# Gated recurrence and mixture of experts on one core: a newly planned order of instructions, wider products, other fillers

## The chip, the cores and the metric

One core of a Trainium2 chip runs the whole program. The metric is the time of one execution on the device, in microseconds (us), as the median of several runs.

## What is computed

```python
# attention: B, H, S, D = 4, 8, 768, 48; complex decay a_re + i a_im, its size held under 0.999
for t in range(S):
    S_re, S_im = ar * S_re - ai * S_im + kv(t), ar * S_im + ai * S_re      # a 48 x 48 state per head
    y[t] = q[t] @ S_re
# experts: x = y as 3072 rows of 384
do = x @ w_skip > 0;  e = argmax(x @ w_gate);  gate = softmax(x @ w_gate)[e]     # 8 experts
out = x + do * gate * (relu(x @ w1[e]) @ w2[e])                            # 384 -> 1024 -> 384
```

## The kernel before

**Attention.** The sequence is cut into 6 chunks of 128 tokens; with 4 batches that gives 24 units (chunk c, batch b), each for all 8 heads. Instead of the recurrence step by step, a unit uses prefix products of the decays. `gates` (L267) takes logarithm, arctangent, exponential and sine on ScalarE, in 7 groups of units (`STARTS`), since these functions need two sets of tables and each change of set is a table load (L790). Its tiles: `tr` is the angle, which TensorE sums over the tokens with a triangular matrix (prefix product `pt`, L331); the sum, in turns, is rounded to whole turns by adding a large constant (the first rounding, `near`, L335, on ScalarE), and VectorE subtracts that (L340) and takes the absolute value (L350), so that sine and cosine (`cs`) have a small argument. `pl` (L366) is the prefix product of the logarithms, and `e` the two exponentials of it. `ready` (L407) multiplies q and k by `e` (L421) and by sine and cosine (`w`, L428), and TensorE transposes the result (`tp`, L436; copied out as `wT`, L445). `unit` (L451) makes the scores `pa` (L477), masks them into `at` (L484), the state product `ps` (L498) that is added to the state `T` (L504), the attention product `py` of scores and state (L519, L522), its copy `yT` and the output product `px` (L536), whose weights `wg` bring the rows back to 384 columns and append eight gate scores and the skip score: 105 columns for each pair of heads.

**Route.** For chunks 0 to 4 `route` (L588) finds the expert of each token and its rank there: VectorE steps, the counts `pr` on TensorE (L605 to L608), and `cand` (L633), which reads the counts back. `pr`, `ps` and `px` take turns in one PSUM bank (`ps_g`): a product for it can start only when the reader of the one before has finished. GpSimd then scatters the rows to a buffer sorted by expert, 224 places for each (L585). The last chunk has a short cut, unit by unit (`route1`, L656): its rows for expert 0 are gathered by products with one-hot tiles (`ohx`, L881), which give `pt` of the expert stage. Two small products (`pg` and `pf`, L391 and L401) carry the chunk's whole decay to the layout of the state; VectorE copies it to `Fall` (L405).

**Experts.** For each expert (`experts`, L855): gather its rows by a load (`xg`, L889), transpose (`pt`, L901), split into a high half `xh` (L907) and a low half `xl` (L911); first layer `ph`, 8 blocks of 128, each with 9 matmuls high by high, high by low and low by high (L925); ReLU on ScalarE (`hh`, L931), its low half on VectorE (`hl`, L935); second layer `po`, for two halves a and b of the rows and 8 blocks, 3 matmuls each (L946 to L948; the last one reads `hl`); scaled result `og` (L954) and a scatter by GpSimd (L958). Weights come by `weights` (L825): seven loads `r` (L841), the cast to a high half on ScalarE (`h`, L848), the subtraction to a low half on VectorE (`l`, L853). Two raw buffers serve the first two experts; a buffer is free when the subtraction has read it. `check` (L975) sets flags for inputs that need a general path; its VectorE steps (L982 to L1003) give `fb`.

**The order.** Every step is put down with its engine, a cost, a due time (in units, moved by a table `SHIFT` of one number for a kind of step), what it needs, and the buffers that it takes and frees. `Plan.order` (L73) goes through them as a list scheduler: it takes the step that can start first on its engine, among equals the one due first, and so writes out the whole program's order for TensorE (P), ScalarE (A), VectorE (V), GpSimd (G) and the loads on SyncE (S). Each engine runs its list strictly in that order. Where TensorE would have a gap before the first attention product, fillers (`warm`, L753, products of 128 by 128 whose result is not used) are put in: as many as the planned gap holds at 0.23, not before `FILL`. `warm` also doubles the cost of TensorE's steps where the plan takes the array for not yet warmed up.

## Time and profile before

| | us |
|---|---|
| median of 3 runs (412.81 to 412.97) | 412.95 |
| profiled execution, its own time | 414.31 |
| its span, first to last instruction | 412.5 |
| TensorE busy (matmuls) | 379.5 (92%) |
| VectorE busy | 317.3 (77%) |
| ScalarE busy | 278.7 (68%) |
| GpSimd busy | 64.3 (16%) |

The profiled execution takes 414.31 us, 1.8 us more than its span. Busy time is an average over stages: up to about 250 us attention, from 267 us on the experts. TensorE's matmuls overlap, so its share is an upper value. The mean granted clock of TensorE is 0.987 of full speed.

### The profile page before, as it was taken

The page shows a single profiled execution, that of the slowest core. Times are in us where ns is not written, and L with a number is a line of the kernel's source. Part 1 is how long each engine was busy: PE and PEld are TensorE (multiplying, and loading weights), DVE is VectorE, ACT ScalarE, POOL GpSimd, SP SyncE. Part 2 cuts the span into 40 slices and gives each one's busy share as a digit, 9 for nine tenths or more (in the row PEclk, how much of TensorE's full clock was granted, in tenths as well). Part 3 has the DMA queues.
Part 4 walks back from the last instruction along what each step waited for, and adds up shares of the span by engine and source line. Part 5 has one row for each costly group of instructions (what it writes and reads, how often), then busy time and mean ns, then how long its engine had stood idle before and what let it go on. Part 6 is the DMA issues. An engine that isn't in the chain of part 4 may idle for free. (4 is left out here: it accounts for less than half of the span.)

```text
span 412.5 us, 9865 instructions
## 1 busy us (share of the span) xinstructions
PE 379.5 (92%) x3742; PEld 341.0 (83%) x3742; DVE 317.3 (77%) x728; ACT 278.7 (68%) x546; POOL 64.3 (16%) x102
## 2 busy tenths in 40 slices
PE   6589999999998999899989988799999999999993
PEld 6377688678797878778968877799899999999992
DVE  5559999999999969988997977959675667757220
ACT  5797999998995799489797664447544656446020
POOL 9100000004004100520040040302112121110101
PEclk9699999999999999999999999999999999999998
DMA  9978969989869737433734765588877767771001
GB/s 157 186 120 163 184 124 167 222 246 224 157 153 203 149 74 167 102 79 70 162 88 118 208 185 173 169 264 272 245 222 225 221 200 241 214 229 64 27 2 35
DMA packets 160758, 67.15 MB, mean 163 GB/s; under 512 B 142310, under 2 KB 156295, under 8 KB 160704
## 3 DMA queue, kind: packets, MB, share of 16 engines
q1 hardware_dynamic: 158144, 61.81, 64.5%
q0 software_dynamic: 2560, 4.63, 3.4%
q8 instruction: 32, 0.52, 0.5%
q14 instruction: 22, 0.18, 0.2%
HBM read 54.24 MB, written 14.98 MB: 168 GB/s over the span
## 5 line engine op out<-in xcount | busy, mean ns | idle before, releaser
L848 ACT CAST h<-r 128x768 fp32r<-128x768 f32 (+1 forms) x56 | 51.1, 925 | 39.6 <-PE po L948 19.3
L853 DVE TENSOR_TENSOR l<-r,h 128x768 fp32r<-128x768 f32 (+1 forms) x56 | 58.8, 1070 | 14.2 <-ACT h L848 14.2
L585 POOL DMA_INDIRECT xs<-xa,sl x24 | 31.3, 1304 | 221.9 <-DVE ain L307 84.4
L436 PE MATMUL tp<-ident,w 128*96 128x128 f32 x384 | 52.2, 275 | 2.4 <-DVE w L428 1.7
L925 PE MATMUL ph<-xh,h 128*128 128x224 f32 x192 | 52.7, 279 | 1.7 <-DVE hl L935 1.4
L445 ACT COPY wT<-tp 96x512 f32<-96x512 f32 x92 | 50.4, 583 | 4.3 <-PE tp L436 4.1
L925 PE MATMUL ph<-xh,l 128*128 128x224 f32 x192 | 51.9, 274 | 0.0
L925 PE MATMUL ph<-xl,h 128*128 128x224 f32 x192 | 50.1, 275 | 0.0
L436 PEld LDWEIGHTS tp<-ident,w 128*96 128x96 f32 x384 | 41.4, 128 | 8.6 <-issue 3.7
L931 ACT ACTIVATE hh<-ph 128x224 fp32r<-128x224 f32 x64 | 22.7, 359 | 33.8 <-PE ph L925 33.8
L428 DVE TENSOR_TENSOR w<-qk,cs 128x768 f32<-128x768 f32 x48 | 44.9, 949 | 0.2
L946 PE MATMUL po<-h,hh 128*112 128x384 f32 x128 | 43.6, 341 | 0.0
L947 PE MATMUL po<-l,hh 128*112 128x384 f32 x128 | 43.1, 337 | 0.0
L948 PE MATMUL po<-h,hl 128*112 128x384 f32 x128 | 43.1, 337 | 0.0
L477 PE MATMUL pa<-wT,wT 96*64 96x128 f32 (+1 forms) x768 | 38.7, 250 | 1.1 <-issue 0.6
L925 PEld LDWEIGHTS ph<-xh,h 128*128 128x128 f32 x192 | 36.8, 192 | 2.8 <-DVE hl L935 2.1
L925 PEld LDWEIGHTS ph<-xh,l 128*128 128x128 f32 x192 | 36.8, 192 | 0.0
L519 PE MATMUL py<-at,vt 128*64 128x128 f32 x192 | 36.3, 279 | 0.6 <-DVE at L484 0.5
L935 DVE SCALAR_TENSOR_TENSOR hl<-ph,hh 128x224 fp32r<-128x224 f32 x64 | 23.6, 383 | 16.4 <-ACT hh L931 16.4
L477 PEld LDWEIGHTS pa<-wT,wT 96*64 96x64 f32 x768 | 34.1, 137 | 2.4 <-issue 1.5
L519 PE MATMUL py<-at,vs 128*64 128x128 f32 x192 | 36.1, 278 | 0.0
L925 PEld LDWEIGHTS ph<-xl,h 128*128 128x128 f32 x192 | 35.5, 192 | 0.0
(170 smaller groups left out, 849.4 us busy)
## 6 DMA issues: line engine op xcount, KB each, us to landing
r<-in_moe_w_dram SPq DMA_DIRECT2D x24, 512.0 KB
r<-in_moe_w_dram SPq DMA_DIRECT2D x32, 384.0 KB
ain<-in_a_re_dram SPq DMA_DIRECT2D x24, 192.0 KB
ain<-in_a_im_dram SPq DMA_DIRECT2D x24, 192.0 KB
qk<-in_q_dram SPq DMA_DIRECT2D x24, 192.0 KB
qk<-in_k_dram SPq DMA_DIRECT2D x24, 192.0 KB
vt<-in_v_dram SPq DMA_DIRECT2D x24, 192.0 KB
out_dram<-xa SPq DMA_DIRECT2D x5, 768.0 KB
```

Of the source, the lines that this page charges most:

```text
L428: V.tensor_tensor(n, X["qk", u][:, k].unsqueeze(2).to_broadcast([128, H, 2, D]), X["cs", c][:, b], ALU.mult)
L436: nc.tensor.transpose(tp[:, h], n[:, hh * 4 + h].rearrange("p k d -> p (k d)"), self.ident)
L445: (V.tensor_copy if onV else A.copy)(X["wT", u, k][:, hh * 4:hh * 4 + 4], X["tp", u, k, hh])
L477: PE.matmul(pa[p, i, t0:], k[:, h, ts], q[:, h, t0:], start=True, stop=True)
L519: PE.matmul(py[j * 64:j * 64 + 64, hp], vs[:, hp] if j else vt[:, 2 * hp], at[:, 2 * hp + j], start=True, stop=(c == 0))
L585: self.nc.gpsimd.indirect_dma_start(out=self.xsv[c * B + b], out_offset=bass.IndirectOffsetOnAxis(ap=sl, axis=0), in_=xa[:, b], in_offset= ...
L848: nc.scalar.copy(X["W", e, n][0][:, ks], X["raw", e, i])
L853: nc.vector.tensor_tensor(lo[:, ks], X["raw", e, i], hi[:, ks], ALU.subtract)
L925: PE.matmul(ph, w[:, k, ks(j)], x[:, k], start=(i == 0), stop=(i == len(terms) - 1))
L946: PE.matmul(po, hh[:, j, ts(t)], w2h[:, j], start=(j == 0), stop=False)
L947: PE.matmul(po, hh[:, j, ts(t)], w2l[:, j], start=False, stop=False)
L948: PE.matmul(po, hl[:, j, ts(t)], w2h[:, j], start=False, stop=(j == NF - 1))
```

## The change

It gives the planner other numbers and a few other rules, and with them a new order of nearly all instructions; and it alters some shapes.

- All constants of the planner are new: lead times of the table sets (`LEADS`, `TRIG`), of the loads and of `ready` (`READY`, `PULL`), the place of the flags (`CHECK`), and `SHIFT`, with 51 entries for 36. The cost of a score product is 0.69 for 0.62.
- Fillers may start at 3.0 instead of 9.0; a gap is counted with 0.7 less instead of 0.25 less, and the first block gets 8 fewer. The doubling of costs for an array not warmed up ends at 6.5 instead of 15.0.
- The state product has 64 columns instead of 48 (the 16 added ones are zeros of the value tile `vt`), the output product 128 instead of 105 (23 columns of zero weights). What is read from their tiles stays the same.
- The first rounding of units 0, 1 and 2 is a VectorE operation instead of one of ScalarE.
- The casts of expert 1's weights wait for the second low half `xl` of expert 0's rows, and are due from n − 0.8 in steps of 0.2, instead of from n − 1.5 in steps of 0.15 (n = 24 units). The weights of expert 0 are spread up to n − 1.25 instead of n − 0.2.
- All four scatters of the first chunk, not the first alone, name the clearing of the buffer as a need.

```diff
@@ -26,15 +26,17 @@
-AHEAD, TRIG, READY, PULL = 3.0, 1.48, 1.28, 2.95
+AHEAD, TRIG, READY, PULL = 3.0, 1.7, 1.02, 3.16
-WAFTER, WGAP, CHECK = 0.41, 0.29, 3
-FETCH = 1.69
-FILL = 9.0
-SHIFT = {'rt4': 1.08, 'xl': 0.32, 'py': -0.87, 're2': -0.04,
...
+WAFTER, WGAP, CHECK = 0.9, 0.32, 0.5
+FETCH = 1.68
+FILL = 3.0
+NV = 3
+EARLY = 1.25
+SHIFT = {'sum': -0.3, 'near': 0.18, 'qe': 1.37, 'eps': 0.48,
...
-LEADS = {0: 7.67, 1: 3.67, 2: 2.09, 3: 2.19, 4: 3.21, 5: 1.9, 6: 1.57, 7: 2.34}
+LEADS = {0: 5.86, 1: 2.7, 2: 1.89, 3: 1.23, 4: 2.34, 5: 2.24, 6: 2.0, 7: 0.84}
@@ -117,7 +119,8 @@
-            n = int((s - max(free["P"], FILL) - 0.25) / 0.23)
+            gap = s - max(free["P"], FILL) - 0.7
+            n = int(gap / 0.23) - 8 * (free["P"] < FILL)
             if e == "P" and n > 0 and ("py", 0, 0) not in end:
                 out.append((max(free["P"], FILL), ("fill", len(out)), lambda n=n: self.fill(n)))
@@ -130,7 +133,7 @@
-                    if s < FILL + 6.0 or warm[1] < 4.0:
+                    if s < 6.5 or warm[1] < 4.0:
                         us *= 2
@@ -212,7 +215,7 @@
-        self.wg = cst.tile([128, H // 2, 2 * D + E + 1], F32, name="wg")
+        self.wg = cst.tile([128, H // 2, 128], F32, name="wg")
@@ -330,9 +333,14 @@
-        @add(("near", u), "A", 0.49, t1, [("pt", u)])
-        def _():
-            A.activation(X["tr", u][:, 1], X["pt", u], AF.Copy, bias=ROUND)
+        onV = u < NV
+
+        @add(("near", u), "V" if onV else "A", 0.55 if onV else 0.49, t1, [("pt", u)])
+        def _():
+            if onV:
+                V.tensor_scalar(X["tr", u][:, 1], X["pt", u], ROUND, None, ALU.add)
+            else:
+                A.activation(X["tr", u][:, 1], X["pt", u], AF.Copy, bias=ROUND)
@@ -465,7 +473,7 @@
-            @add(("pa", u, hh), "P", 0.62, t, [("wT", u, k, hh) for k in range(2)], take=[("pa", u, hh)], free=[("wT1", u)])
+            @add(("pa", u, hh), "P", 0.69, t, [("wT", u, k, hh) for k in range(2)], take=[("pa", u, hh)], free=[("wT1", u)])
@@ -493,17 +501,17 @@
-                ps = X["ps", u] = self.ps_g.tile([96, H, D], F32, name=f"ps_{nm}", tag="g")
+                ps = X["ps", u] = self.ps_g.tile([96, H, 64], F32, name=f"ps_{nm}", tag="g")
                 for h in range(H):
-                    PE.matmul(ps[:, h], X["w", u, 1][:, h].rearrange("p k d -> p (k d)"), X["vt", u][0][:, h, 0:D], start=True, stop=True)
+                    PE.matmul(ps[:, h], X["w", u, 1][:, h].rearrange("p k d -> p (k d)"), X["vt", u][0][:, h], start=True, stop=True)
...
-                    V.tensor_tensor(T, X["Sb", u][:, :, 0:D], X["ps", u], ALU.add)
+                    V.tensor_tensor(T, X["Sb", u][:, :, 0:D], X["ps", u][:, :, 0:D], ALU.add)
@@ -528,9 +536,9 @@
-        @add(("px", u), "P", 0.925, t, [("yT", u), ("wg", 0)], take=[bank], free=[("yT", u)])
-        def _():
-            xs = [H // 2, 2 * D + E + 1]
+        @add(("px", u), "P", 0.95, t, [("yT", u), ("wg", 0)], take=[bank], free=[("yT", u)])
+        def _():
+            xs = [H // 2, 128]
...
@@ -639,7 +647,8 @@
-            steps[20] += (("zero", 4),)
+            for i in range(20, 20 + B):
+                steps[i] += (("zero", 4),)
@@ -818,11 +827,11 @@
-        gap = (n - 0.2 - t) / 8
+        gap = (n - EARLY - t) / 8
         self.weights(0, t, gap, gone, end)
         self.experts()
 
-    def weights(self, e, t, gap, need=(), begin=None):
+    def weights(self, e, t, gap, need=(), begin=None, hold=()):
@@ -840,7 +849,7 @@
-            @add(("wh", e, i), "A", 1.05 if i < KD else 0.835, t + gap * (i + 0.4), [("wd", e, i)] + old)
+            @add(("wh", e, i), "A", 1.05 if i < KD else 0.835, t + gap * (i + 0.4), [("wd", e, i)] + old + list(hold))
@@ -862,7 +871,7 @@
-        self.weights(1, n - 1.5, 0.15, [("w", u, 1)])
+        self.weights(1, n - 0.8, 0.2, [("w", u, 1)], hold=[(None, ("xl", 0, 1))])
```

Left out of the diff: the columns of `wg` and of the output product are named up to 105 where they are loaded and summed. In the trace every 32-bit product of attention is two matmuls, so that a filler counts twice there; in the lists below it counts once.

**TensorE, start of the program.** `pt` and `pl` are the prefix products of units 0, 1, 2, `tp` the first transposes. Before:

```order
L753 MATMUL warm<-turns 128x128 x22
L331 MATMUL pt_269<-tr_202,turns 128x384
L331 MATMUL pt_276<-tr_211,turns 128x384
L753 MATMUL warm<-turns 128x128
L331 MATMUL pt_285<-tr_223,turns 128x384
L366 MATMUL pl_295<-U_221,mask 128x384
L753 MATMUL warm<-turns 128x128
L366 MATMUL pl_308<-U_235,mask 128x384
L753 MATMUL warm<-turns 128x128 x16
L366 MATMUL pl_350<-U_242,mask 128x384
L753 MATMUL warm<-turns 128x128 x5
```

After:

```order
L762 MATMUL warm<-turns 128x128 x38
L334 MATMUL pt_289<-tr_202,turns 128x384
L334 MATMUL pt_292<-tr_211,turns 128x384
L334 MATMUL pt_297<-tr_223,turns 128x384
L374 MATMUL pl_311<-U_221,mask 128x384
L374 MATMUL pl_323<-U_235,mask 128x384
L762 MATMUL warm<-turns 128x128 x10
L374 MATMUL pl_351<-U_242,mask 128x384
L762 MATMUL warm<-turns 128x128
L444 MATMUL tp_0_0_370<-ident,w_0_359 96x128 x4
```

The first block of fillers grows from 22 to 38, the three `pt` stand together, and no filler stands between `pt` and `pl`.

**TensorE, after the counts of the third chunk** (`pr`, the last of its products). Before:

```order
L608 MATMUL pr_2310<-oh_2211,ones 128x8
L436 MATMUL tp_14_0_2316<-ident,w_14_2188 96x128 x4
L436 MATMUL tp_14_1_2325<-ident,w_14_2188 96x128 x4
L536 MATMUL px_0_2337<-wg,yT_0_2290 128x105 x4
L436 MATMUL tp_15_0_2353<-ident,w_15_2295 96x128 x4
L436 MATMUL tp_15_1_2363<-ident,w_15_2295 96x128 x4
```

After (left out: the scores `pa`, six rows):

```order
L616 MATMUL pr_2187<-oh_2155,ones 128x8
L444 MATMUL tp_13_1_2194<-ident,w_13_2099 96x128 x4
L485 MATMUL pa_162<-wT_12_1996,wT_12_2086 64x128
...
L444 MATMUL tp_14_0_2241<-ident,w_14_2168 96x128 x4
L444 MATMUL tp_14_1_2250<-ident,w_14_2168 96x128 x4
L506 MATMUL ps_1_2260<-vt_158,w_13_2099 96x64 x8
L527 MATMUL py_0_2279<-at_0_2271,vt_156 64x128
```

The next product for the bank of the counts was `px`, behind two transposes; it is now the state product `ps`, behind three half transposes and both scores.

**VectorE, last routing steps and first expert** (`todo` is the last step of the routing; `Fall` belongs to `pf`). Before:

```order
L718 SCALAR_TENSOR_TENSOR todo<-m_3_3651 128x1
L853 TENSOR_TENSOR l_1_3737<-r_1_2_3748,h_1_3736 128x1024
L405 COPY Fall<-pf_3693 96x32
L911 TENSOR_TENSOR xl_3775<-pt_0_3728,xh_3774 128x3x112
L911 TENSOR_TENSOR xl_3775<-pt_1_3732,xh_3774 128x3x112
L982 MEMSET ok 128x384
L995 TENSOR_SCALAR ok<-Fall 96x192
L996 TENSOR_SCALAR ok<-Fall 96x192
L853 TENSOR_TENSOR l_1_3783<-r_1_3_3764,h_1_3782 128x768
L935 SCALAR_TENSOR_TENSOR hl_3817<-ph_0_3785,hh_3816 128x224
```

After (left out: seven further steps of the flags):

```order
L727 SCALAR_TENSOR_TENSOR todo<-m_3_3658 128x1
L991 MEMSET ok 128x384
L1004 TENSOR_SCALAR ok<-Fall 96x192
L1005 TENSOR_SCALAR ok<-Fall 96x192
...
L1011 TENSOR_REDUCE fl<-todo 128x1
L920 TENSOR_TENSOR xl_3766<-pt_0_3722,xh_3765 128x3x112
L920 TENSOR_TENSOR xl_3766<-pt_1_3726,xh_3765 128x3x112
L1012 TENSOR_TENSOR fb<-fb,fl 128x1
L862 TENSOR_TENSOR l_1_3775<-r_1_0_3720,h_1_3774 128x1024
L862 TENSOR_TENSOR l_1_3775<-r_1_1_3730,h_1_3774 128x1024
L944 SCALAR_TENSOR_TENSOR hl_3807<-ph_0_3778,hh_3806 128x224
```

The subtractions `l_1` of expert 1's weights went behind the low halves `xl`, the flags (`ok` to `fl`) ahead of them, and `Fall` stands several steps earlier. In the same place of ScalarE's list the casts of the third and fourth part of expert 1's weights stand between the activations of blocks 3 and 4 of expert 0, where they were ahead of the first block; on SyncE's list the loads of these parts stand behind three gathers `xg` instead of ahead of them; and on TensorE `pg` and `pf` stand ahead of the last gathers by product, not between them and the first `ph`.

In the experts TensorE's list ran through the blocks of the first layer and then through those of the second; now second-layer products stand among them, for instance `ph` 4 and 5, `po` a3, a4, b0, a5, b1, `ph` 6, `po` b2, b3, a6, `ph` 7, and the last five products of the program are b4, b5, a7, b6, b7, so that the two results `og` are ready one right after the other.

## Rows read from the trace of the kernel before

**Rows 1.** Busy time of each engine by stretch (start:end, length; us and instructions), clock, DMA.

```profile
25.36:60.00 34.64, 32.02 (x310) 26.04 (x311) 34.22 (x66) 32.16 (x65) 0.00 (x0) 1.00 0.86 150
60.00:140.00 80.00, 76.30 (x927) 64.47 (x924) 76.40 (x183) 71.61 (x144) 10.28 (x10) 1.00 0.90 196
140.00:240.00 100.00, 95.53 (x1164) 81.94 (x1163) 87.94 (x212) 80.22 (x160) 14.58 (x11) 1.00 0.52 120
...
300.00:405.40 105.40, 105.38 (x771) 104.31 (x769) 60.68 (x105) 45.74 (x90) 15.11 (x17) 1.00 0.53 160
```

**Rows 2.** The same view, of shorter stretches; granted clock behind the engines.

```profile
13.00:19.80 6.80, 4.80 (x9) 2.89 (x10) 2.54 (x6) 4.76 (x10) 0.00 (x0) 0.50 1.44 187
...
252.00:258.00 6.00, 4.14 (x53) 3.84 (x52) 4.00 (x24) 2.84 (x5) 0.97 (x1) 1.00 0.60 195
```

**Rows 3.** Timeline of TensorE at the start: start, length, line, tiles, [idle before].

```profile
2.74 6.79 PE L753 MATMUL warm<-turns 128*128 128x128 f32 x44 [2.74 <-POOL turns L170]
14.99 2.93 PE L331 MATMUL pt<-tr,turns 128*128 128x384 f32 x4 [5.47 <-ACT tr L260]
...
21.61 3.73 PE L753 MATMUL warm<-turns 128*128 128x128 f32 x32
...
38.70 0.91 PE L331 MATMUL pt<-tr,turns 128*128 128x384 f32 x2 [0.15 <-ACT tr L260]
```

**Rows 4.** Timeline of VectorE at the start.

```profile
17.29 0.61 DVE L340 SCALAR_TENSOR_TENSOR tr<-tr,col,pt 128x384 f32<-128x384 f32 x1 [3.59 <-ACT tr L335]
18.01 0.36 DVE L350 TENSOR_SCALAR tr<-tr 128x384 int32<-128x384 int32 x1
...
25.36 0.56 DVE L293 TENSOR_TENSOR tr<-ain,tr 128x384 f32<-128x384 f32 x1 [4.08 <-ACT tr L260]
...
28.30 0.55 DVE L307 SCALAR_TENSOR_TENSOR ain<-ain,tr 128x384 f32<-128x384 f32 x1
```

**Rows 5.** Timeline of ScalarE at the start.

```profile
22.01 1.28 ACT L790 ACT_TABLE_LOAD   x1
```

**Rows 6.** Timeline of TensorE: state product, output product, scores.

```profile
44.27 1.56 PE L498 MATMUL ps<-vt,w 128*96 128x48 f32 x16 [0.18 <-DVE T L506]
...
241.70 1.04 PE L536 MATMUL px<-wg,yT 128*128 128x105 f32 x8
...
123.93 1.55 PE L477 MATMUL pa<-wT,wT 96*64 96x64 f32 x32
```

**Rows 7.** Waits of TensorE: engine, line, awaited operation: us in total, times, longest.

```profile
PE px L536 <- DVE cand L633: 2.0, 2, 1.4
...
PE ph L925 <- DVE hl L935: 1.4, 2, 0.9
```

**Rows 8.** Timelines of VectorE, TensorE, SyncE and ScalarE, from attention to experts.

```profile
262.06 1.22 DVE L853 TENSOR_TENSOR l<-r,h 128x1024 fp32r<-128x1024 f32 x1
...
263.99 1.56 PE L881 MATMUL pt<-early,xa 128*128 128x112 f32 x12 [0.18 <-DVE ohs L680]
...
266.79 0.37 PE L925 MATMUL ph<-xh,h 128*128 128x224 f32 x1 [0.32 <-ACT xh L907]
...
271.39 16.88 SPq L841 DMA_DIRECT2D r<-in_moe_w_dram  x11
...
277.57 0.83 ACT L848 CAST h<-r 128x768 fp32r<-128x768 f32 x1 [2.03 <-DMA r<-in_moe_w_dram]
```

**Rows 9.** Timelines of TensorE and VectorE, last block of the last expert.

```profile
396.73 0.27 PE L925 MATMUL ph<-xh,l 128*128 128x224 f32 x1
...
397.44 0.39 DVE L935 SCALAR_TENSOR_TENSOR hl<-ph,hh 128x224 fp32r<-128x224 f32 x1 [0.61 <-ACT hh L931]
```

**Rows 10.** Timelines of VectorE and GpSimd at the end.

```profile
401.23 0.62 DVE L954 SCALAR_TENSOR_TENSOR og<-po,xg 112x384 f32<-112x384 f32 x1 [3.40 <-PE po L948]
405.42 0.62 DVE L954 SCALAR_TENSOR_TENSOR og<-po,xg 112x384 f32<-112x384 f32 x1 [3.57 <-PE po L948]
...
406.31 0.94 POOL L958 DMA_INDIRECT out_dram<-og,idx  x1 [2.73 <-DVEq L1014]
```

8 lines of the change are left out of this document (4 added, 4 removed).

## The prediction

> **What bounds the kernel now.** I read the busy time of each engine by stretch first. From 25 to 60 us VectorE works 34.22 of 34.64 us, from 60 to 140 it works 76.40 of 80 and TensorE 76.30; from 140 to 240 TensorE leads with 95.53 of 100; in the experts from 300 to 405.4 TensorE has 105.38 of 105.40 [rows 1]. So the attention is held by two engines, VectorE a little more in its first half, TensorE in its second, and the experts by TensorE alone: there only what shortens TensorE's own list, or takes a wait from it, can pay. The change shortens no list; its matmuls, vector operations and transfers keep their number but for 12 fewer filler matmuls and three roundings that change engine. What can move is therefore waiting, and that I read next: the start, where no engine is full; the waits of TensorE (the view of waits); the hand-over from attention to experts; the end. The chain of waits that ended last names only GpSimd here and tells nothing of the stages.
>
> Everything is summed against the profiled execution's own 414.31 us. The median of the runs, 412.95, lies 1.36 us below that, and I take 1.36 off at the end.
>
> **The start.** In the kernel before, 44 fillers run from 2.74 for 6.79 us, and the first prefix product, which follows, begins at 14.99 after 5.47 us without work [rows 3]; between 13 and 19.8 us the granted clock is 0.50, its level of 1.2 GHz [rows 2]. Four instructions of the product take 2.93 us there, two at full clock 0.91 [rows 3]. The change issues 76 instead of 44: 32 more at the 3.73 us that 32 took at full clock [rows 3] end at 2.74 + 6.79 + 3.73 = 13.3 us, 1.7 us before the product. A stretch of 6 us with 1.86 us of idle TensorE kept clock 1.00 [rows 2], so I expect full clock through the start. The added fillers cost nothing: nothing else is ready for TensorE before 14.99.
>
> What that buys hangs on VectorE, since the first rounding of units 0 to 2 moves there from ScalarE, in front of the other two steps of the unit. Those two start 0.72 us apart, and the second takes 0.36 [rows 4]. The rounding on VectorE has no row; it reads the same PSUM tile as the 0.61 us operation and does as little as the 0.36 us one [rows 4], which are its bounds. I take 0.5, because the PSUM read makes it nearer the former. A unit then takes 0.5 + 0.72 + 0.33 = 1.55 us, with a little overlap of the last. The first product should end at 14.99 + 0.91 = 15.9; three units end at 15.9 + 0.1 + 4.65 = 20.65, the last cosine 0.7 later, and ScalarE's table load begins at 21.35 instead of 22.01 [rows 5]: 0.65 sooner (0.3 to 1.0 by the bounds).
>
> Behind the load ScalarE now makes four exponentials in a row and VectorE does the product with the first of them before it turns to the next unit's gates; in the kernel before it waited 4.08 us until 25.36 for those gates, and four rows of work (two of the gates, two of the product) were done at 28.30 [rows 4]. Now it resumes at about 23.75 with 1.9 us of product, the gates follow at 25.7, and all four are done near 26.85: 1.45 us sooner. TensorE and ScalarE are also above 90% busy up to 60 us [rows 1], so I do not carry all of it through: **−0.9 us**, bounds 0 and −2.5 (the second if the shorter chain and the half-clock stretch of 6.8 us [rows 2] both count in full).
>
> **Wider products.** The trace shows each product of the program as two matmuls. The 320 matmuls of the state go from 48 to 64 columns, the 192 of the output from 105 to 128. I divide a group's time, less the 0.25 us that one such matmul lasts (0.27 in [rows 9]), by its number less one. State: 1.31/15 = 87 ns. Output: 0.79/7 = 113 ns. Fillers of 128 by 128 [rows 3]: 3.48/31 = 112 ns. A product of 64 columns with only 64 columns of weights: 1.30/31 = 42 ns [rows 6]. So 105 columns step like 128, and 64 columns can pass in 42 ns where the state's step is 87: the weights set the step and the added columns are hidden under their load. **0 us**; if they were not, 16 × 320 + 23 × 192 columns at 42/64 ns cost 6.3 us, the upper end. The Trainium skill's page "TensorE: Matmul & The Clock Gate", section "Back-to-back issue gap", gives an isolated matmul a time that grows with its columns, N/2.4 + 2.5 ns; by it 9,536 added columns would cost 4.0 us, and the sum would be above the time before. The rows speak for the load in its place. The copies that read these tiles keep their sizes.
>
> **Waits on the single PSUM bank.** Route counts, state and output product share one bank. TensorE waited 2.0 us in two places for VectorE to read the counts before it could write an output product, 1.4 the longest [rows 7]. The new order puts scores, transposes and, at one of the two, an attention product between the counts and the next use of the bank, which at the other is a state product; so VectorE has time. The shorter of the two lies before 140 us, where VectorE is no less full, and I count nothing for it; the longer lies where TensorE leads, and a part will come back at the next wait: **−1.1 us**, bounds +1 (the state product now meets the same bank earlier) and −2.0.
>
> **Into the experts.** In the kernel before, three subtractions for expert 1's weights, 1.22 us each, stand among the routing steps of the last chunk on VectorE. The last gather on TensorE, which needs the routing, starts at 263.99, is released by VectorE, and the first expert product begins 1.24 us after its end, at 266.79, behind two small products of the state's decay [rows 8]. The subtractions now follow the first expert's inputs, and the small products go before the gather. Two subtractions less would release the gather 2.3 us sooner; the gather before it, for which only one less counts, then holds it, so that I take 1.4. The gather's end is then 264.1, the cast of the inputs and a wake-up take about 0.85, and the first expert product begins at 264.95, 1.85 us sooner.
>
> What is late next: the error flags, some 2.3 us of short steps on VectorE, now stand ahead of the low halves of the inputs, which the last three matmuls of the first block need; that block waits about 0.55 us. The first second-layer product waits an estimated 0.1 for its own low half, behind the moved subtractions. The third and fourth loads for expert 1 now stand behind the gathers on SP's queue, and their buffers come free only by the moved subtractions. A load issued there at 271.39 kept ScalarE until 277.57, 6.2 us [rows 8]; issued near 268.4 it lands at 274.6, the next an estimated 1 us later. ScalarE casts both, and VectorE subtracts both, ahead of the activation of block 4, whose second-layer product TensorE reaches near 276.8, while that chain ends near 277.8: 1.0 us of waiting. The wait for a low half in this stretch, 1.4 − 0.9 = 0.5 us [rows 7], goes. −1.85 + 0.55 + 0.1 + 1.0 − 0.5 = −0.7, taken as **−0.6 us** for such steps as I have not seen, bounds −1.6 (the loads land in time) and +2.5 (each 3 us later).
>
> **The experts.** First- and second-layer products are now interleaved. The longest wait for a low half, 0.9 us [rows 7], goes. A low half is ready 1.0 us after TensorE has taken its block's last matmul (396.73 and a step of 0.11, against 397.44 + 0.39) [rows 9]; the new order often leaves just two second-layer products, 2 × 3 matmuls at some 0.175 us, in between, and it is only the third matmul of the next that reads it. I let this give back 0.05 us in each of eight experts: **−0.5 us**, bounds −0.9 and +2. At the very end both results are read back to back, where they were 4.2 us apart, and the second scatter, 0.94 us of GpSimd [rows 10], may stand behind the first: **+0.2 us**, bounds 0 and +0.94.
>
> **Sum.** −0.9 + 0 − 1.1 − 0.6 − 0.5 + 0.2 = −2.9 us: 411.4 against the profiled 414.31, or 410.1 us against the median.
>
> **Rivals.** A: *expert 1's weights arrive late.* ScalarE and VectorE keep strict order, so a late third load blocks block 4's activation, then its low half, then TensorE. For it: the load now waits for the subtraction and for three gathers, and 6.2 us was its time there. Against: TensorE has about 12 us of products before it needs that block. Each us that the loads land after 274.6 is one more; at 278 the wait is 4.4, and with 0.4 more from the tight low halves it eats the gains: 410.1 + 3.4 + 0.4 = 413.9. Chance 0.20. B: *the gains cancel*: VectorE, full until 140 us, swallows the start and a new wait on the bank replaces the old one; −0.9 and −1.1 go, −0.9 remains at best: 412.1 to 413.5. Chance 0.13. C: *the new order frees more*: the other waits of attention, some of the 4.5 us in which TensorE has nothing in 140 to 240 and 3.7 in 60 to 140 [rows 1], go as well, 2.5 us further: 407.6. Chance 0.15. D: *the added columns are paid*: at the 42 ns per 64 columns they cost 6.3 us in full, half of that where VectorE covers it: 410.1 + 3.1 = 413.2 and up to 416.4. Chance 0.05, since [rows 6] speak against it. [...] That the change does not do what it says is no case here: the new rows stand in the order of the program.
>
> **How the numbers follow.** The forecast itself has 0.47. About 0.83 us (0.2%) can be told from no change. Forecast and C, nearly all, are faster: 0.61. B and the edges of the others give 0.14 to no change, A and D and their edges 0.25 to slower. The range goes from 406.8 (C with more of the start's bound) to 414.3 (A); the likeliest case alone spans 408.9 to 411.6.
>
> **What would show it.** Right: granted clock 1.00 from 13 to 20 us, table load near 21.4, VectorE back at work near 23.8; state products still stepping by 87 ns and output products by 112; no wait of an output product for the counts above 0.5 us; first expert product near 263 to 264 (all the earlier gains included); in the experts no wait above 0.3 us but one near block 4 of expert 0. Wrong: a half-clock stretch anywhere, a wait of several us for a weight load in expert 0, or state products above 95 ns.

## The result and the profile after

| | us |
|---|---|
| changed kernel, median of 20 runs (412.82 to 420.56, and one of 529.37) | 415.61 |
| kernel before on the same chip, median of 20 runs (411.53 to 414.1) | 412.12 |
| ratio | 1.0076, interval 1.0054 to 1.0097 |
| profiled execution of the changed kernel, its own time | 414.82 |
| its span, first to last instruction | 413.0 |

The ratio leaves out the changed kernel's three runs in a slower state (420.24, 420.56 and 529.37 us), so that it is below the quotient of the two medians.

The change makes the kernel 0.5 to 1.0% slower where I forecast 0.7% faster; 415.61 lies outside the range of 406.8 to 414.3. The profiled execution of before, 414.31, was itself 1.4 to 2.2 us above that kernel's two medians (412.95 and 412.12), so the two profiles differ by less than the medians do.

Busy time by stretch in the changed kernel, in the columns of [rows 1] and [rows 2]:

```profile
13.00:19.80 6.80, 4.31 (x8) 1.69 (x8) 4.20 (x9) 4.79 (x9) 0.00 (x0) 0.73 1.07 182
25.00:60.00 35.00, 28.76 (x291) 22.57 (x290) 34.41 (x68) 32.43 (x65) 0.00 (x0) 1.00 0.87 156
60.00:140.00 80.00, 76.08 (x924) 64.20 (x920) 75.22 (x179) 69.12 (x139) 11.56 (x10) 1.00 0.86 186
140.00:240.00 100.00, 95.25 (x1150) 81.28 (x1149) 89.21 (x214) 79.65 (x160) 10.76 (x10) 1.00 0.54 122
300.00:405.40 105.40, 105.40 (x778) 105.01 (x778) 63.09 (x108) 50.52 (x95) 15.87 (x16) 1.00 0.55 175
```

In the experts TensorE is as full as before. From 25 to 60 us it works 28.76 of 35.00, where it was 32.02 of 34.64 [rows 1], while VectorE stays full. This difference is fillers, which took 5.71 us of that stretch before (42 matmuls) and take 2.27 now (14); without them TensorE works some 26.3 us before and 26.5 after. And the granted clock from 13 to 19.8 us is 0.73, not the 1.00 that I expected, although the 38 fillers are there: they end at 12.95, the product follows after 2.00 us without work, the clock falls at 16.08 and is back at 22.91.

Starts of TensorE, VectorE and ScalarE (each a timeline; columns as in [rows 3]):

```profile
2.73 10.22 PE L762 MATMUL warm<-turns 128*128 128x128 f32 x76 [2.73 <-POOL turns L173]
14.95 1.85 PE L334 MATMUL pt<-tr,turns 128*128 128x384 f32 x4 [2.00 <-ACT tr L263]
...
28.13 1.54 PE L506 MATMUL ps<-vt,w 128*96 128x64 f32 x16 [0.91 <-issue]
```

```profile
15.90 0.56 DVE L341 TENSOR_SCALAR tr<-pt 128x384 f32<-128x384 f32 x1 [2.25 <-PE pt L334]
...
24.14 0.96 DVE L429 TENSOR_TENSOR qk<-qk,e 128x768 f32<-128x768 f32 x1 [3.53 <-ACT e L263]
```

```profile
21.29 1.28 ACT L799 ACT_TABLE_LOAD   x1
22.59 1.99 ACT L263 ACTIVATE e<-pl,col 128x384 f32<-128x384 f32 x4
```

The rounding on VectorE takes 0.56 us (taken as 0.5), the table load begins at 21.29 (worked out as 21.35; 22.01 in [rows 5]), VectorE is back at 24.14 (worked out as 23.75; 25.36 in [rows 4]). So far the start goes as worked out.

The waits of TensorE in the whole program (as [rows 7], the longest entries and those of the experts):

```profile
PE ps L506 <- ACT xa L560: 3.0, 5, 1.3
PE warm L762 <- POOL turns L173: 2.7, 1, 2.7
PE py L527 <- DVE at L492: 2.6, 3, 1.4
PE pt L334 <- ACT tr L263: 2.5, 2, 2.0
PE pa L485 <- DVE wT L453: 2.0, 2, 1.1
PE pa L485 <- ACT wT L453: 1.6, 2, 0.9
PE ph L934 <- DVE xl L920: 1.2, 1, 1.2
...
PE px L544 <- ACT yT L535: 1.0, 3, 0.7
PE px L544 <- ACT xa L560: 1.0, 1, 1.0
...
PE po L957 <- DVE hl L944: 0.5, 1, 0.5
```

The wait for the counts `cand`, 2.0 us in [rows 7], is gone. In its place, on the same bank, state and output products wait for `xa`, ScalarE's copy of the output product, which has to empty the bank: 3.0 and 1.0 us. Scores and attention products wait for `wT` and `at`; in the kernel before each of these entries is 0.5 us or less:

```profile
PE pa L477 <- DVE wT L445: 0.5, 1, 0.5
PE py L519 <- DVE at L484: 0.5, 1, 0.5
```

VectorE in turn waits longer for the state products (the same view for VectorE, before and after):

```profile
DVE T L504 <- PE ps L498: 3.1, 4, 1.3
```

```profile
DVE T L512 <- PE ps L506: 5.5, 5, 3.0
```

Into the experts (timelines of TensorE, SyncE and ScalarE) and the end (VectorE and GpSimd):

```profile
265.67 0.37 PE L934 MATMUL ph<-xh,h 128*128 128x224 f32 x1 [0.53 <-ACT xh L916]
```

```profile
268.95 10.77 SPq L850 DMA_DIRECT2D r<-in_moe_w_dram  x4
```

```profile
276.15 1.05 ACT L857 CAST h<-r 128x1024 fp32r<-128x1024 f32 x1 [1.06 <-DMA r<-in_moe_w_dram]
...
278.50 0.61 ACT L940 ACTIVATE hh<-ph 128x224 fp32r<-128x224 f32 x2
```

```profile
404.65 0.62 DVE L963 SCALAR_TENSOR_TENSOR og<-po,xg 112x384 f32<-112x384 f32 x1 [0.80 <-PE po L957]
405.71 0.62 DVE L963 SCALAR_TENSOR_TENSOR og<-po,xg 112x384 f32<-112x384 f32 x1 [0.44 <-PE po L957]
```

```profile
407.31 0.94 POOL L967 DMA_INDIRECT out_dram<-og,idx  x1 [0.30 <-issue]
```

The first expert product starts at 265.67, 1.1 us sooner than 266.79 [rows 8]; I had it near 263 to 264.

### The profile page after: what moved, and what is told of

Same layout as the page of the kernel before. It is cut to its first block, busy times and chain, and to the rows that moved or that the text cites. A ratio compares the mean times of both kernels' runs of the same rounds, so it can differ in the third digit from the quotient of the medians.

```text
span 413.0 us, 9847 instructions
## 1 busy us (share of the span) xinstructions
PE 379.9 (92%) x3730; PEld 339.6 (82%) x3730; DVE 319.2 (77%) x731; ACT 278.8 (68%) x543; POOL 63.5 (15%) x102
## 4 chain that ended last, share of the span: by engine, by line
DVE 35%; PE 35%; DMA 11%; ACT 10%; issue 6%; SPq 1%; POOL 0%; DVEq 0%; POOLq 0%; ACTq 0%
PE ph L934 12%; DMA r<-in_moe_w_dram 6%; DVE w L436 6%; PE po L957 4%; PE po L956 4%; PE po L955 4%; DVE at L492 4%; DVE qk L429 3%; PE ps L506 3%; DVE tr L348 2%; DVE ain L310 2%; DMA row<-tr 2%; DVE tr L296 2%; DVE U L319 2%; ACT h L857 2%
## 5 line engine op out<-in xcount | busy, mean ns | idle before, releaser
L857 ACT CAST h<-r 128x768 fp32r<-128x768 f32 (+1 forms) x56 | 50.9, 927 | 35.4 <-DMA r<-in_moe_w_dram 18.7
L593 POOL DMA_INDIRECT xs<-xa,sl x24 | 28.5, 1188 | 222.6 <-DVE w L436 79.5
L506 PEld LDWEIGHTS ps<-vt,w 128*96 128x96 f32 x320 | 29.1, 165 | 10.5 <-ACT xa L560 5.9
```

The costliest lines, as they stand in the source:

```text
L506: PE.matmul(ps[:, h], X["w", u, 1][:, h].rearrange("p k d -> p (k d)"), X["vt", u][0][:, h], start=True, stop=True)
L857: nc.scalar.copy(X["W", e, n][0][:, ks], X["raw", e, i])
```

## Experiments

The letters in the expectations: O, the new order of start and attention loses the time; W, the new plan for expert 1's weights does; C, the added columns do (rival D of the prediction); K, the clock falls because fillers are missing. Where parts of the program have the old list and others the new, the kernel makes both lists and joins them behind a named step (in short; `old` and `new` stand for the two sets of constants and rules, and e5, e6, e7, e10 and e11 write the join out for two lists):

```diff
-            self.order = self.plan.order()
+            both = []
+            for j, P in enumerate(PLANS):      # old or new constants and rules
+                globals().update(P)
...
+                two = self.plan.order()
+                go = [x for i, x in enumerate(two) if (x[1][0] == "fill" and i > on) or (x[1][0] != "fill" and x[1] not in had)]
+                if j < len(CUTS):
+                    go = go[:[x[1] for x in go].index(CUTS[j]) + 1]
+                both += go
```

```diff
+PLANS, CUTS = [old, new], [("px", 22)]                      # e5, e11
+PLANS, CUTS = [new, old], [("px", 22)]                      # e6
+PLANS, CUTS = [new, old], [("LE", 2)]                       # e7, e10
+PLANS, CUTS = [new, old, new], [("LE", 1), ("px", 22)]      # e13, e18
+PLANS, CUTS = [new, old, new], [("e1", 2), ("px", 22)]      # e14
+PLANS, CUTS = [old, new], [("px", 0)]                       # e15
+PLANS, CUTS = [old, new], [("px", 11)]                      # e16
+PLANS, CUTS = [new, old, new], [("px", 9), ("px", 22)]      # e17
```

`LE` 1 and 2 are the second and third load of the exponential's tables, with the loads of the other set the third and fifth table load of the program (21.29 and 46.94 us in the changed kernel); `e1` is the second exponential of a unit. With its constants a list brings its rules along: the place of the first rounding, the spread of expert 0's weights and the needs of the first scatters were not tested apart from it, but for the rounding (e13).

A join can cost something that neither list has, so that a joined kernel that is not slow tells more than one that is. "Marks" are the starts of the output products, px_0 to px_23, one for each unit, and of the first expert product, ph_0; they repeat within some 0.1 us between profiles of one list over long stretches, but shift at half clock and in some places without it. A list can also have done more of the later units' work at the same mark, so that a mark shows a loss only where the work behind it is the same. Ratios are to the kernel before, run beside each; its medians went from 412.12 to 414.61 us, so that times of different experiments are not to be set against each other.

**e1_again**: the changed kernel, unaltered.

> The changed kernel once more, unaltered, for a second profile and to see whether its times scatter again. The first runs gave 415.6 us in the middle, from 412.8 to 420.6, where the kernel before kept between 411.5 and 414.1. Theory W (the weights of expert 1 come late, or TensorE's clock falls for lack of work where the experts begin): a scatter of 5 us or more again, ratio near 1.008, and the second profile differs from the first between 265 and 300 us. Theory O (the new order of attention is slower in itself): ratio near 1.008 with the last output product again 1 to 2 us later than before's 258.07. If it was a disturbance of that chip: ratio within 0.2% of 1, scatter as before's.

416.63 us, 1.0122 [1.0084, 1.0161]. Its marks are those of the first profile until 38 us; then

```profile
37.90:41.40 3.50, 3.50 (x20) 2.56 (x20) 2.96 (x6) 2.18 (x5) 0.00 (x0) 0.51 1.13 206
```

in the view by stretch, where the first profile has clock 1.00, and px_1 starts at 59.19 instead of 57.66. So one list shows half-clock stretches at different places, and this one cost 1.53 us there; at px_5 0.33 of it is left, at px_11 0.68.

**e2_old_weights**: the old plan for expert 1's weights in the changed kernel.

```diff
-        self.weights(1, n - 0.8, 0.2, [("w", u, 1)], hold=[(None, ("xl", 0, 1))])
+        self.weights(1, n - 1.5, 0.15, [("w", u, 1)])
```

> The changed kernel with one line put back: the weights of expert 1 planned as before (due from n - 1.5 in steps of 0.15, no hold). Attention keeps the new order row for row up to the last units; the subtractions and loads for expert 1 stand early again. Theory W: the scatter shrinks to about 2 us and the median falls by 2 to 4 us, to 412 to 413. Theory O: it falls by under 1 us. Theory C (the added columns cost time): it stays at 415.

418.74 us, 1.0156 [1.0124, 1.0189]. No better, where W had 412 to 413; and slower than any of the theories had it. The weights' new plan is not what makes the changed kernel slow.

**e3_hold_alone**: the reverse, the line with `hold` in the kernel before.

> The kernel before with the new plan for the weights of expert 1 alone (due from n - 0.8, steps of 0.2, casts held until the second low half of expert 0's rows). Attention keeps the old order. Theory W: slower by 2 to 4 us (415 to 416), scatter of 5 us or more, waits for the weight loads near the start of the experts. Theories O and C: within 0.8 us of 412.1.

414.63 us, 1.0053 [1.0033, 1.0073]: 2.3 us slower, as W had it (2 to 4) and O and C had not. In the old list the hold does cost time; that it costs none with the new way into the experts, e5 shows below. ph_0 comes at 262.53, 2.35 us sooner than in the next kernel, which has the old plan for these weights (a part of it because that one has a half-clock stretch at 256.4 to 259.8 us), and the last `og` at 403.93, 0.34 us later than there. The experts begin sooner, as worked out, and the time is given back within them (this profile is of the fastest of its nine runs, 412.91 us); so the hold by itself does not pay.

**e4_wide_alone**: the kernel before with the wider products alone.

```diff
-                ps = X["ps", u] = self.ps_g.tile([96, H, D], F32, name=f"ps_{nm}", tag="g")
+                ps = X["ps", u] = self.ps_g.tile([96, H, 64], F32, name=f"ps_{nm}", tag="g")
...
-            xs = [H // 2, 2 * D + E + 1]
+            xs = [H // 2, 128]
```

> The kernel before with the wider state and output products alone, order and all else kept. Theory C: 4.0 us slower by the rate of a matmul without its weight load, up to 6.3; the state product's step goes from 87 to 95 ns or more. My reading of the rows: within 0.2%, steps of 87 and 112 ns as before. Theories W and O: no difference.

412.29 us, 0.9997 [0.9979, 1.0014]. The columns are free within 0.2%: C falls.

**e5_old_attention**, and once more on another chip as **e11_old_attention_again**: the old list up to px_22, then the new one; all else as changed.

> Two orders joined: up to the output product of unit 22 every engine follows the order of the kernel before (start and rounding of the kernel before too, wide products), from there on the order of the changed kernel (held weights of expert 1, flags ahead, interleaved experts). Theory O (the new order of attention is where the time is lost, 2.5 to 3.3 us by the marks of the profiles): 411 to 412.5 us, no slower than before. Theory W (held weights and the clock at the hand-over): 414 to 415, as with the hold alone (414.6).

> The version of e5 again (old order to the output product of unit 22, new order behind it), for a narrower interval: e5 gave 0.9978 [0.9954, 1.0001]. If the new hand-over and experts gain what their marks show (last result 0.9 us sooner): ratio 0.9975 to 0.9985. If e5 was chance: within 0.1% of 1.

413.02 us, 0.9978 [0.9954, 1.0001], and 413.23 us, 0.9981 [0.9955, 1.0006]. The new way into the experts (the hold with it), their list and the end don't lose; by these medians they gain some 0.2%, with intervals that end at about zero. (The last `og` is at 402.71 in e5, 404.27 in e11 and 403.59 in e4; e11 and e4 have a half-clock stretch late in their profiles, so the marks don't settle a difference of this size.) The loss lies before them.

**e6_new_attention**: the new list up to px_22, then the old one.

> The other half: start and attention of the changed kernel up to the output product of unit 22, then hand-over and experts in the order of the kernel before. Theory O: 414.5 to 416, the output product of unit 23 some 3 us later than with the old order. Theory W: 412 to 413.

417.8 us, 1.0088 [1.0055, 1.0121]. The whole loss is there with the old experts: O. This profile has clock 0.50 in another place again,

```profile
94.40:101.10 6.70, 6.70 (x52) 6.20 (x51) 4.40 (x9) 4.62 (x10) 1.77 (x3) 0.50 0.85 178
```

and px_5 starts 3.87 us later than in the changed kernel, 3.57 of which are left at px_11; behind that, from px_11 to px_12, 1.77 us come on top at full clock (see e12).

**e7_new_start**: the new list up to the third load of the exponential's tables, then the old one. (The expectation puts this load near 35 us; in the trace that is a load of the other set, and the named one is at 48.48, between px_0 and px_1.) **e10_start_filled**: the same with seven more fillers in each of its last three groups of fillers.

> The start of the changed kernel alone (38 fillers first, three roundings on VectorE, four exponentials in a row), up to the second load of the exponential tables near 35 us; from there the order of the kernel before to the end, with the wide products. My term for the start, -0.9 us: 411.2. If the rest of attention swallows the start (rival B): 412.0 to 412.6. If new waits arise at the seam: 413 or more; then the marks of the output products show where.

> The new start with the old order behind it (as e7), with seven more fillers in each of the last three groups before the first attention product, where TensorE was busy 8.3 of 13.7 us from 24.2 to 37.9. Theory K (the clock falls after that stretch because the fillers end): the profile shows no half-clock stretch near 38 to 41 us, the second output product comes 1.5 us sooner than e7's 61.05, and the ratio to the kernel before falls from e7's 1.0028 to 1.000 or below. Against it: the ratio stays near 1.003, and the start is slower for its order alone.

415.42 us, 1.0028 [1.0004, 1.0051], and 417.46 us, 1.0060 [1.0034, 1.0087]. By stretch, e7 and then e10:

```profile
24.00:60.00 36.00, 28.67 (x258) 21.86 (x260) 32.48 (x61) 31.12 (x62) 0.00 (x0) 0.95 0.86 152
```

```profile
24.00:60.00 36.00, 31.38 (x298) 25.24 (x300) 32.47 (x61) 31.19 (x62) 0.00 (x0) 1.00 0.85 150
```

px_0 is 9.7 us sooner in e7 than in e4 and px_1 2.2 later; VectorE has 3.5 us without work in this stretch. In e10 the clock is 1.00 here and in the whole of attention, and px_1 is no sooner (61.18, 61.05 in e7). K falls for this place. But the loss can't be put down to the new start either: in the changed kernel, which goes on with the new list, px_1 starts at 57.66, sooner than in the kernel before (58.87), and VectorE in e17, which keeps the new list to px_9, has only 0.89 us without work from 24 to 60. So what e7 and e10 lose here lies, as far as this shows, at the join.

**e8_px_other_bank**: output products in the two banks of the prefix products.

```diff
-            px = X["px", u] = self.bank(f"px_{nm}", xs) if late else self.ps_g.tile([128] + xs, F32, name=f"px_{nm}", tag="g")
+            px = X["px", u] = self.bank(f"px_{nm}", xs)
```

> The changed kernel in its own order, but the output product of every unit takes one of the two banks of the prefix products instead of the single bank that it shares with state product and counts. Theory B1 (the loss in attention comes from that bank: state products wait 3.0 us in five places for the copy of an output product, and VectorE 5.5 us for state products): 2 to 4 us faster than the changed kernel, 412 to 414, and that wait is gone. If the order loses its time elsewhere: within 1 us of the changed kernel, 415 to 417; if the prefix products now wait instead, the waits show them.

423.23 us, 1.0189 [1.0145, 1.0233]. The wait for `xa` moves with the output product:

```profile
PE pt L334 <- ACT xa L560: 2.8, 3, 1.0
...
PE pl L374 <- ACT xa L560: 2.3, 2, 1.5
```

With it come four stretches at half clock before the end (two in the changed kernel), so that the run doesn't price the bank. Up to px_9, where it has only the stretch at the start as the changed kernel has, it is 0.8 us later than that (136.01, 135.21), not sooner as B1 had it. It shows that what waits for `xa` is whatever shares a bank with the output product.

**e9_one_more_tr** and, beside it, **e12_changed_again**, unaltered. One buffer more for the angles `tr`: in the changed kernel a state product at 93 us waits for a copy into `xa`, and ScalarE comes to that copy late because it waits for a transfer out of a buffer of `tr`.

```diff
-            tr = X["tr", u] = self.fe.tile([128, 2, H, D], F32, name=f"tr_{u}", tag="tr", bufs=self.rooms["tr"])
+            tr = X["tr", u] = self.fe.tile([128, 2, H, D], F32, name=f"tr_{u}", tag="tr", bufs=self.rooms["tr"] + 1)
```

> The changed kernel in its own order, with a sixth buffer for the angle tile. In its profile ScalarE waited at 92.19 us for a buffer that a small copy of a last row still read; that copy stood on SyncE's queue behind four clearings of the sorted buffer, and behind the waiting operation on ScalarE stood the copy that frees the bank for a state product (TensorE idle 1.46 us before 93.55). If such chains are where the new order loses: that wait is gone, the tenth output product comes 1 to 2 us sooner than 135.2, and the kernel is 0.8 to 2 us faster than the changed one on the same chip. If VectorE's order sets the time there: within 0.5 us of it.

> The changed kernel once more, as the neighbour of e9 on the same chip: ratio 1.007 to 1.012, as before. Its profile is a third execution of one order: up to the first half-clock stretch that differs it should repeat the marks of the first to within 0.1 us, and lose 1 to 3.5 us behind each such stretch that falls into attention.

417.84 us, 1.0060 [1.0026, 1.0094], and 416.84 us, 1.0050 [1.0024, 1.0076], below the 1.007 to 1.012 that I expected of e12. px_5 comes 1.1 us sooner in e9 (96.29, 97.40 after), px_9 does not (135.09, 135.21). This wait removed is swallowed within four units.

e12 shows a second source of scatter. Its marks are those of e1 up to px_11 (152.75, 152.67 in e1), with a half-clock stretch in nearly the same place; px_12 then starts at 169.14, 167.19 in e1, at full clock in both. In e12 TensorE breaks off within a score product, with nothing to wait for that the trace shows ("issue"):

```profile
167.69 0.22 PE L485 MATMUL pa<-wT,wT 96*64 96x64 f32 x1 [0.40 <-issue]
168.42 0.66 PE L485 MATMUL pa<-wT,wT 96*64 96x64 f32 x7 [0.52 <-issue]
```

and ScalarE stands still at the same time:

```profile
168.51 0.58 ACT L535 COPY yT<-py 128x512 f32<-128x512 f32 x1 [1.86 <-remote]
```

e6, e8 and e9 have the same, the changed kernel's first profile, e1, e2 and e15 do not. What it is was not found.

**e13_rounding_alone**, on another chip **e18_rounding_alone_again**: e5, with the new list also up to the second load of the exponential's tables, that is the 38 fillers and the rounding on VectorE. **e14_start_longer**: the same up to the exponentials of unit 2.

> The kernel with the old attention and the new experts (two measurements before, 0.9978 and 0.9981), with one more part of the change: the new list up to the second table load, so 38 fillers at the start and the first rounding of units 0 to 2 on VectorE; the old list from there to the end of attention. Three theories of the loss in the new start. P (the later part of the new start pushes units 1 and on back for unit 0): this part is harmless, table load near 21.3 us, px_1 within 0.5 us of 58.9, ratio 0.996 to 0.999. V (the rounding is a load too much on VectorE, which is full to 60 us): px_1 1 us or more later, ratio 1.000 or above. F (more fillers cost granted clock later on): a half-clock stretch between 24 and 60 us in the profile and px_1 1 us or more later.

> The best version so far once more, on the same chip as the run before it: the old attention behind the second table load, the start with 38 fillers and the first rounding on VectorE, the new experts. 0.9955 to 0.999; above 1.000 its first measurement (0.9973) was a matter of the chip.

> As the one before, but the new list runs on until the exponentials of unit 2 (four exponentials in a row on ScalarE behind the table load, VectorE going on with their product). P: ratio as the one before or up to 0.002 above it, px_0 and px_1 both near the old marks, since unit 0 is not yet drawn ahead. If the four exponentials in a row are what delays units 1 and 2: px_1 1 us or more later and ratio 1.000 or above.

411.12 us, 0.9973 [0.9951, 0.9994]; 412.94 us, 0.9953 [0.9928, 0.9977]; e14 412.19 us, 0.9994 [0.9973, 1.0016]. The start by itself does no harm, as P had it, and e13 is faster than both kernels, in both measurements. How much of that is the start can't be told: px_1 at 58.17 against 58.15 and 58.56 in e5 and e11, whose own table loads are at 21.33 and 21.73.

**e15_old_start**: the old list up to px_0, then the new one. **e16_old_half**: the old list up to px_11. **e17_new_half**: the new list up to px_9, the old to px_22, then the new one.

> The changed kernel with the old list up to the first output product (51 us) and the new one from there to the end. It tells how the loss is shared between the start and the rest of attention. All of the loss in the start: ratio 0.998, px_9 to px_23 as in the kernel with the old attention. Shared, as the kernel with the new start alone (1.0028) against the whole (1.005 to 1.012) suggests: 1.002 to 1.005. All of it behind px_0: 1.005 or above.

> The changed kernel with the old list up to the output product of unit 11 (154 us) and the new one from there. The waits on the copy of x and the longer spans between table loads lie before 154 us, the wait for the counts that the change removes (1.4 us) lies behind it. If the loss is in the first half alone: ratio 0.995 to 0.998 and no worse than the kernel with the old attention throughout (0.998). If the new second half loses too (px_11 to px_23 lasts 2.1 us longer in the changed kernel than in the old order, with routing steps done earlier in it): 1.000 to 1.003.

> The counterpart of the kernel with the old first half: the new list from the start to the output product of unit 9 (135 us), the old list from there to the end of attention, the new experts. If the loss sits behind px_11 alone (old first half 1.007, old attention throughout 0.998): 0.997 to 1.000, with px_21 within 1 us of the kernel with the old attention (240.4). If the first half loses by itself as well (px_9 was 2.7 us and px_11 -2.2, px_12 +1.0 us off the old marks, so some 1 to 1.5 us): 1.001 to 1.004, with px_21 1 us or more later. If the two halves' losses do not add (the first half's is absorbed by the waits of the second): as the whole change, 1.005 or above, only where the second half is new too, so here near 1.000.

418.49 us, 1.0130 [1.0095, 1.0165]; 415.12 us, 1.0070 [1.0051, 1.0089]; 415.84 us, 1.0042 [1.0013, 1.0071]. All three are slow. e15, with the old start, is no faster than the changed kernel, so the loss lies behind px_0 or at its join. Each half of the new attention is slow where it is joined to the old one, the second too, in which the removed wait lies; e16 lies above both of its forecasts. Over e5 the two halves lose 0.9 and 0.6%, together as much as the largest loss of the whole (0.7 to 1.4%), so that a part of them may belong to the joins. e14 and e17 had clock 1.00 from 9 us to the end of the experts in their profiles, and so can be set side by side without the clock. From 24 us to ph_0, e14 and then e17:

```profile
24.00:262.46 238.46, 224.01 (x2650) 191.66 (x2650) 217.84 (x554) 194.29 (x391) 37.49 (x29) 1.00 0.69 155
```

```profile
24.00:267.24 243.24, 222.09 (x2622) 188.18 (x2622) 219.09 (x554) 194.55 (x391) 35.15 (x29) 1.00 0.68 152
```

VectorE has the same 554 instructions and works 1.25 us more, TensorE 28 fewer, all of them fillers, and 1.92 us less; the stretch is 4.78 us longer, of which 3.17 are left at the last `og` (405.68, 402.51). TensorE is without work for 238.46 − 224.01 = 14.45 us in e14 and 21.15 in e17 (18.7 in the changed kernel); 3.44 of the 6.70 more stand where e14 has fillers (5.71 us, 2.27 in e17). Which waits these are, e14 and then e17 in the view of waits:

```profile
PE px L549 <- DVE cand L646: 2.0, 2, 1.4
...
PE tp L449 <- DVE w L441: 1.1, 2, 0.8
...
PE px L549 <- ACT xa L565: 0.2, 1, 0.2
```

```profile
PE tp L449 <- DVE w L441: 3.3, 5, 0.9
...
PE ps L511 <- ACT xa L565: 2.3, 3, 1.9
...
PE pa L490 <- DVE wT L458: 2.0, 2, 1.1
PE pa L490 <- ACT wT L458: 1.9, 2, 1.3
...
PE px L549 <- DVE T L517: 1.5, 2, 1.3
```

The changed kernel itself, without a join, can be set beside e14 too, up to px_22, since its clock is 1.00 from 22.91 to 268.67 us. e14, then the changed kernel, from 24 us to the start of px_22:

```profile
24.00:247.32 223.32, 211.88 (x2526) 180.34 (x2526) 206.12 (x475) 190.40 (x380) 33.72 (x25) 1.00 0.70 154
```

```profile
24.00:252.36 228.36, 211.15 (x2512) 177.65 (x2510) 208.60 (x484) 190.74 (x381) 27.90 (x25) 1.00 0.71 152
```

5.04 us more at full clock, with nine more VectorE steps (2.48 us) done by then. At px_9 the changed kernel is 3.18 us behind e14 (135.21, 132.03), at px_11 1.73 ahead (151.99, 153.72): the marks don't tell in which half it loses.

## Why the prediction was wrong

**The start.** The worked steps came: rounding 0.56 us, table load 0.72 us sooner, VectorE back 1.22 us sooner. What failed is the step from there to the end, "I do not carry all of it through: −0.9 us". Against other executions the table load was hardly sooner at all: with the old start it lies at 21.33 to 22.05, by where the half-clock stretch falls, and I had read one execution. And I followed the new list only to 27 us. Behind it unit 0 is drawn ahead: px_0 comes 11.31 us sooner than before, px_1 1.21 sooner, and px_2 is already 1.11 late (64.81, 63.70 before). e13 and e14, whose new part ends before px_0, lose nothing; e7 and e10, whose new part ends between px_0 and px_1, lose 0.3 to 0.6%, but as far as shown at their join. So no run shows the −0.9, and none shows that the start loses by itself. The expected clock of 1.00 between 13 and 20 us did not come in this profile, though it did in nine of thirteen with the same 38 fillers. It was worth nothing either: px_0 is at 39.68 with the half-clock stretch of 6.8 us, and at 39.73 to 39.84 without one (e2, e9, e17); my bound of −2.5 had counted it.

**Wider products, 0 us.** Right. e4 measures 0.9997 with an interval of 0.2% to either side; a state group takes 1.54 us with 64 columns, 1.56 with 48 [rows 6]. The Trainium skill's "TensorE: Matmul & The Clock Gate", section "Back-to-back issue gap", gives the time of an isolated matmul by its columns, by which I estimated 4.0 us; the section itself says that in a stream of weight loads and matmuls both set the spacing, and that this formula is too low for few columns. The trace agrees with that: the median step from one state product to the next is 85 ns with 48 and with 64 columns, and 112 ns for output products with 105 and with 128. The upper end of e4 is 0.6 us (0.14% of 412.3).

**The single bank, −1.1 us.** This is the step that failed most. The named wait went, as said. But I looked at two places of an attention in which nearly all instructions move, and put every other place at nothing, without a reason. The bank is freed by ScalarE's copy as well as by the counts, and the new order meets that copy late: 4.0 us of waits for `xa` (3.1 in e1) for 2.0 of `cand`. I had the mechanism as a bound, "+1 (the state product now meets the same bank earlier)", and in rival B, whose price stopped at no gain. The attention as a whole lost some 0.7 to 1.4% (e5 and e11 at 0.998 against 1.005 to 1.012 for the unaltered list), 3 to 6 us. What the runs show is that the new list of attention, behind the start of e13, is the cause: with the old one in its place the loss is gone (e5, e11, e13, e18), with the new one and the old experts it is there (e6). In which waits it appears, the views show; that the bank's waits are the larger part is argued only, since e8 failed to price them, and e9 shows that one wait less need not bring anything. What in the list costs the time stays open.

**Into the experts, −0.6; experts −0.5; end +0.2: together −0.9 us.** The sum agrees: e5 and e11 are at −0.2%, that is 0.8 to 0.9 us, though an interval of that width doesn't exclude zero. The parts were partly off. From px_22 to ph_0 it is 14.71 us in e5 and 15.14 in e14, where it was 16.60 before: 1.5 to 1.9 us sooner, against 1.85 worked out. From ph_0 to the last `og` it is 139.12 and 140.05, where it was 138.63: the experts' −0.5 is not to be seen, they give back 0.5 to 1.4 us of what the way into them gained. The first block waited 1.2 us for its low half, behind the flags, not 0.55. Expert 1's third load came 7.2 us after its issue (276.15 against 268.95; 6.2 taken), and the activations of blocks 4 and 5 began at 278.50; yet TensorE waits only 0.5 us in all for a low half `hl` in the whole program, and that at 291 us, where I had 1.0 near block 4 (0.4 there in e14, at full clock; in this profile the half-clock stretch from 268.67 may hide some). The results `og` are 1.06 us apart and the last scatter starts 1.00 later than before, with TensorE's end.

**The rivals.** A did not come: the late loads stopped next to nothing. D fell with e4. C, that the order frees more, did not come either. B came nearest, with the right mechanism and the wrong size. No rival said that a new order of a stretch with two nearly full engines loses, and that was the missing one: [rows 1] show VectorE at 76.40 and TensorE at 76.30 of 80 us, and there, as I now read it, a shift makes one wait for the other; no run tests this reading by itself.

**The clock** is not settled. Half-clock stretches between 24 and 250 us stand in five of the twelve profiles with the new attention list in any part beyond e14's (e1, e7 and e12 at 37 to 41 us, e6 at 94 to 101, e8) and in none of the eight others. They may be a part of the loss and of its scatter from run to run, but they are not the whole: at clock 1.00 from 24 us on, px_22 starts at 252.36, 253.27 and 253.89 us with the new list (the changed kernel, e2, e9) and at 247.32 to 250.83 with the old one (e5, e11, e13, e14, e18); and e10 and e17 are slow at full clock in their profiles. For the first 60 us the place of the stretch goes with when the same 38 fillers end. In four profiles (the changed kernel, e6, e8, e13) they end at 12.83 to 12.95, TensorE then has nothing for 1.90 to 2.12 us, and the clock falls at 15.83 to 16.08. In nine they end at 13.34 to 14.43, nothing is done for 0.55 to 1.74 us, and there is no fall there; of these, e12, e7 and e1, with the new list and 13.34 to 13.61, have theirs at 37.37 to 37.94, and e2, e9 and e17, with the same list and 14.34 to 14.43, have none before 250. e10 ends its first fillers at 14.31, so that its full clock need not come from the fillers added. What places the later stretches was not found.

## What to carry to other kernels

When a planner writes a new order, the few places that one reads are not the change: where two engines are nearly full, price the whole stretch, with a loss as likely as a gain, and ask of each removed wait what holds the same buffer next. A gain at the start is worth what reaches the second and third unit, not the first (here 11.3 us sooner, then 1.2 sooner, then 1.1 later). And keep the parts of such a change apart: here the new start up to the second load of the exponential's tables and the new experts with the old attention (e13) ran at 0.9973 and 0.9953 of the time before, the whole at 1.005 to 1.012.

## What was not expected of the hardware

The granted clock is not a property of the list: the same instructions showed half clock at 16.08 to 22.91 and 268.67 to 272.08, at 37.94 to 41.35, and at 37.37 to 40.79 us in three profiles. What a stretch costs depends on its place: one of 3.4 us cost 1.5 us at the next mark and 0.7 ten units on (e1), one of 6.8 us 3.9 and then 3.6 six units on (e6), and one of 6.8 us in the start nothing at px_0. Full clock from 9 us to the end of the experts, in turn, went with a slow kernel (e10) as well as with one level with the kernel before (e14). And one list lost 1.9 us between px_11 and px_12 at full clock in some executions and not in others (e12, e1).
